# Fused attention, soft mixture and MLP on one core: logits by 256-token products, a zero block written once, w2 in 4 KB pieces, and another order of the stages

## The chip, the cores and the metric

One Trainium2 chip, one core. The metric is the device time of one execution in microseconds (us), lower is better. The kernel before took 661.55 us (median of 3 runs, 656.04 to 662.62).

## The reference

Three layers in a row, in float32. All shapes are fixed: 8 batches, 8 heads, 576 positions, head width 64, so 4608 tokens of width 512; the mixture has 8 experts with 4 slots each (32 slots).

```python
k_p = k.reshape(B, H, 72, 8, D).mean(3); v_p = v.reshape(B, H, 72, 8, D).mean(3)
attn = softmax(q @ k_p.T / 8)                 # 576 x 72 for each batch and head
x = (attn @ v_p) as (4608, 512)
logits = x @ phi                              # 4608 x 32
d = softmax(logits, axis=0)                   # over the tokens
slot_input = d.T @ x                          # 32 x 512, 4 slots for each of 8 experts
slot_out[e] = relu(slot_input[e] @ w1[e]) @ w2[e]
x = softmax(logits, axis=1) @ slot_out
out = (s * relu(x @ w_in) ** 2 + b) @ w_out   # width 2048 inside
```

## The kernel before, in words

The order on every engine is written out by hand; each engine runs its own list from front to back. Strings at the top of the file (`LOOP`, `FIRST`, `TAIL`, `BEHIND`, `PLAN1`, `PLAN2`, `KEEP`) hold that order.

**Attention loop (L703).** The 4608 tokens are 36 tiles of 128, nine for each pair of batches; tile 0 of nine (jj = 0) takes the last 64 tokens of both batches. Letters stand for steps of a tile, and a string for each pass names which step of which tile comes when: A transposes q (L363), B makes the scores (L387) and takes the row maximum off (L391, L393), C does exp and the normalisation (L401 on ACT, L402 on DVE, L422 on POOL), D transposes the probabilities P (L441, and L449 for the last 64 of the 576 rows), E makes the logits (L467), F transposes them back (L480) and writes them into L (L488). x is never formed: the logits are P times `vpf`, which is the pooled v times phi (576 rows x 32 slots, as four blocks of 128 rows and one of 64). E and F work once for two tiles, on 256 tokens, so 16 times, and once for each jj = 0 tile, so 4 times.

- Step E before: four quarters of 64 tokens, five blocks of rows. Each of the 20 products has a 128 x 32 weight (`vpf`) and 64 moving columns, and quarter g writes partitions 32g to 32g + 31. A float32 product is two matmul instructions, and each has its own weight load, so the trace counts 40 and 40. ACT copies 128 x 64 out (L471), one transpose brings it back (L480), two DVE copies put it into L (L488).
- The fifth block of `vpf` has 64 empty rows, which a POOL memset (L332, in `v_prep3`) clears for each pair of batches.
- `p` in a string advances `prep`, which pools k and v of the next pair (`PLAN1`, `PLAN2`: `k` or `v`, `d` for DVE or `g` for POOL, and the chunk; a capital is a transpose, L275), then L316, L336 and L305. `r` advances `dispatch`, the softmax over the tokens of one batch and its slot inputs (L539 to L614: a maximum by L539, L546 and L548, the difference by L551 and L553, exp at L555, products at L579, transposes at L594, L601 and L606). `w5` is five warm-up products on a constant (L252).

**Tail (L768).** The last steps and the last two dispatches (`6` and `7`), with the merging of the eight batches (`m`, M2, M3, M4), in the order of `TAIL`. It ends with L616, which writes the slot inputs `siz`.

**Expert stage (L975).** 32 pieces of 1 MB, half an expert each, in the order `EORD`: w1 products at L984 (32 slot columns as weight, 256 moving columns of w1, four column groups), w2 products at L993. `hidden` copies the sums (L948), transposes them (L954) and applies relu (L961). `BEHIND` says what is put behind which piece: `t` transposes combine weights (L932, and copies on ACT at L936), `c` their halves, `i` and `o` start a conversion of a block of w_in or w_out to the narrower format (`narrow`, L818: five DVE steps L825 to L835, L837 on ACT, L838 and L839 on POOL). A conversion is advanced by one stage behind each following piece, and its ACT step stands in ACT's list where that happens.

All loads are issued by SP in one order (`pump`), each when a buffer is free. `KEEP` says behind which pieces a ring buffer is kept as scratch, not given back.

**End of the expert stage (L1030).** The slot sums are copied (L1033), transposed in one go (L1034), and copied out of the one PSUM bank by ACT and DVE, two quarters each (L1036).

**MLP (L1212).** 96 steps, each with 18 products of 512 columns at L1139 and, for a later step, two at L1079. In the last group the sums are added into `part` by DVE (L1152), six tiles for a block, and SP writes them out (L1155).

Of the kernel before, what the change touches and what calls it, by code (L numbers as in the profile page):

```python
# [10 lines left out]
F32 = mybir.dt.float32  # L11
# [3 lines left out]
ALU = mybir.AluOpType  # L15
AX = mybir.AxisListType
# [3 lines left out]
WIPOS, WOPOS = 26, 26  # L20


BEHIND = {12: 't0 c3 t1', 20: 'o1', 9: 'c0 c1', 17: 'i1', 16: 't2', 18: 'o0 t3', 15: 'i0', 23: 't4', 10: 'c2', 28: 't5'}
TAIL = "6 C4 D2 F0 E2 X1 6 W3 6 6 6 F2 D3 m D4 W1 6 E4 6 m 7 m 7 F4 7 W2 7 7 M2 6 7 7 X2 M3 6 M4 W3 7 X3 7"
BUSY = 2
CUT = 1

LOOP = (
# [9 lines left out]
)  # L38
FIRST = {
# [8 lines left out]
}  # L48
PREP = (4, 10, 19)
PLAN1 = "kd1 kg0|kg0|kg2|K0 kd1 kg2 vg0|vg0 K1 vg2|vg2 K2 V0 vd1 vd1|V1 V2"  # L50
PLAN2 = "kg2|kg2 kg0|kg0 kg1 K2||kg1|vg2 vg2 K0|vg0|vg0 K1|V2 vg1 V0 vg1|V1"
NRING, NRAW = 10, 3
LTB = 1
KEEP = (1, 4, 6, 7)
XR = (3, 2, 1, 2)

W_MAX = 122879.9921875
# [3 lines left out]
def kernel(  # L61
# [23 lines left out]
    NG = 6  # L85
# [6 lines left out]
    ident = cpool.tile([128, 128], F32, name="ident")  # L92
# [19 lines left out]
    def plan(key, shape_str, src, n, **kw):  # L112
        loads.append((key, shape_str, src, n, kw))
# [74 lines left out]
    for w, e, hf in EORD[:BRIEF] + EORD[BRIEF + NBRIEF:NSLOT] + EORD[BRIEF:BRIEF + NBRIEF] + EORD[NSLOT:]:  # L188

        if (w, e, hf) == EORD[WIPOS]:  # L190
            plan_wi(0)
        if (w, e, hf) == EORD[WOPOS]:
            plan_wo(0)
        if w == "w1":
            plan((w, e, hf), "p (c f) -> p c f", w1[e, 256 * hf:256 * hf + 256, :].rearrange("(c p) f -> p c f", p=128), 2048, c=2)
        else:
            plan((w, e, hf), "p (c d) -> p c d", w2[e, 512 * hf:512 * hf + 512, :].rearrange("(c p) d -> p c d", p=128), 2048, c=4)
    for n in (1, 2):
        plan_wi(n)
    for n in (1, 2):  # L200
# [7 lines left out]
    ap1 = actx.enter_context(tc.tile_pool(name="ap1", bufs=1, side="right"))  # L208
# [43 lines left out]
            nc.tensor.matmul(out=ps[:, 0:128], lhsT=ident, rhs=ident, start=True, stop=True)  # L252

    vt_t, vps_t, vpf_t = {}, {}, {}
    kvp = {}

    def pool_chunk(nm, pr, c, eng):
# [69 lines left out]

    def v_prep3(pr):
        vpt = vpt_t.pop(pr)
        vpf = (ap1 if pr % 2 else apb).tile([128, 5, 2, 32], F32, tag="vpf", name="vpf")  # L330
        vpf_t[pr] = vpf
        nc.gpsimd.memset(vpf[64:128, 4], 0.0)  # L332
        ps = bank()
        for c in range(5):
            n = min(128, PQ - 128 * c)
            nc.tensor.transpose(out=ps[0:n, 64 * c:64 * c + 64], in_=vpt[:, 128 * c:128 * c + n], identity=ident[0:64, 0:64])  # L336
        nc.scalar.copy(out=vpf[:, 0:4], in_=ps[:, 0:256].rearrange("p (c b s) -> p c b s", c=4, b=2))
        nc.scalar.copy(out=vpf[0:64, 4], in_=ps[0:64, 256:320].rearrange("p (b s) -> p b s", b=2))
# [117 lines left out]
    def st_E(t):  # L456
        pr, jj = divmod(t, 9)
        if not place(t)[1]:
            return
        assert held.pop()[1] == t  # L460
        vpf = vpf_t[pr]
        ps = bank()
        quarters = [(bb, t, bb) for bb in range(2)] if jj == 0 else [(0 if jj < 5 else 1, t - 1 + g // 2, g % 2) for g in range(4)]
        for c in range(5):
            for g, (bb, u, y) in enumerate(quarters):
                z = PT[:, c, u % 3, 64 * y:64 * y + 64] if c < 4 else PT4[:, 64 * g:64 * g + 64]
                nc.tensor.matmul(out=ps[32 * g:32 * g + 32, 0:64], lhsT=vpf[:, c, bb, :], rhs=z, start=(c == 0), stop=(c == 4))  # L467
        n = 32 * len(quarters)
        LT = apc.tile([128, 64], F32, tag="LT", name="LT", bufs=LTB)
        LT_t[t] = LT  # L470
        nc.scalar.copy(out=LT[0:n], in_=ps[0:n, 0:64])  # L471

    def st_F(t):
        pr, jj = divmod(t, 9)
        if not place(t)[1]:
            return
        L = L_t[pr]
        n = 64 if jj == 0 else 128
        ps = bank()
        nc.tensor.transpose(out=ps[0:64, 0:n], in_=LT_t.pop(t)[0:n], identity=ident[0:n, 0:n])  # L480
        for y in range(2):
            r = slice(64 * y, 64 * y + 64)
            if jj == 0:
                nc.vector.tensor_copy(
                    out=L[r, 5 * y:5 * y + 6:5, :], in_=ps[0:64, 32 * y:32 * y + 32].unsqueeze(1).to_broadcast([64, 2, 32])
                )
            else:
                nc.vector.tensor_copy(  # L488
                    out=L[r, SLOT[jj] - 1:SLOT[jj] + 1, :], in_=ps[0:64, 0:128].rearrange("p (x y s) -> p y x s", x=2, y=2)[:, y]
                )  # L490


    def merge_1():
# [481 lines left out]
    for n_, key in enumerate(EORD):  # L975
        w_, e, hf = key
        g, ge = divmod(e, EG)
        w = where[key][2]
        if w_ == "w1":
            for c in range(2):  # L980
                kc = 2 * hf + c
                wc = w[:, c].rearrange("p (i c f) -> p c i f", i=2, c=4)
                for x in range(4):
                    nc.tensor.matmul(  # L984
                        out=l1[g][32 * x:32 * x + 32, 0:256],
                        lhsT=siz[:, 128 * e + 32 * kc:128 * e + 32 * kc + 32],
                        rhs=wc[:, x],
                        start=(ge == 0 and kc == 0), stop=(ge == EG - 1 and kc == 3),
                    )
        else:  # L990
            for c in range(4):
                for x in range(4):
                    nc.tensor.matmul(  # L993
                        out=so_ps[32 * x:32 * x + 32, 0:128],
                        lhsT=h1z_of(g, 4 * hf + c)[:, 36 * ge + 16 - 4 * e:36 * ge + 48 - 4 * e],
                        rhs=w[:, c, 128 * x:128 * x + 128],
                        start=(e == 0 and hf == 0 and c == 0), stop=(e == E - 1 and hf == 1 and c == 3),
                    )
        done(key, sum(n_ >= x for x in KEEP))
        if n_ == BRIEF + NBRIEF - 1:  # L1000
            brctx.close()
# [12 lines left out]
        for x in BEHIND.get(n_, "").split():
            f = int(x[1:])
            if x[0] in "ct":
                next((combine_hl if x[0] == "c" else combine_t)(f))
            else:
                todo.appendleft(conv_wi(f) if x[0] == "i" else islice(wo_[f], 2))
        if key != EORD[-1]:  # L1020
            step_convs()
# [6 lines left out]

    busy(l1[1][:, 0:128], BUSY)
    so = si_all[:, 0].rearrange("p c s -> p (c s)")  # L1030
    sot_ps = ps_1.tile([128, 4, 32], F32, tag="hps", name="sot_ps")
    sot = cv.tile([128, 4, 4, 32], F32, name="sot")
    nc.scalar.copy(out=so, in_=so_ps[:, 0:128])  # L1033
    nc.tensor.transpose(out=sot_ps.rearrange("p c s -> p (c s)"), in_=so, identity=ident)  # L1034
    for x, copy in enumerate((nc.scalar.copy, nc.vector.tensor_copy)):
        copy(out=sot[:, 2 * x:2 * x + 2], in_=sot_ps[:, 2 * x:2 * x + 2].unsqueeze(2).to_broadcast([128, 2, 4, 32]))  # L1036
    while convs:
        advance(convs)
    ectx.close()
# [241 lines left out]
```

## Time and profile before

| | |
|---|---|
| median of 3 runs | 661.55 us (656.04 to 662.62) |
| profiled execution | 662.91 us |
| its span (first to last instruction) | 661.1 us |
| mean granted TensorE clock | 0.984 of full |
| busy share of the span: PE, PE weight loads, DVE, ACT, POOL | 94%, 78%, 69%, 61%, 45% |

The profile is of one execution. The 1.8 us between its span and its time lie outside the instructions. PE is the matmul side of TensorE and PEld its weight loads. "Idle before" is time in which an engine stood still ahead of an instruction, with the instruction that released it; "issue" means that nothing in the profile had to be waited for.

### The profile page before, as it was taken

The numbers are of one execution on the slowest core, as the hardware profiler recorded it, in microseconds if no ns is written. First come the engines' busy times: TensorE is split into PE (matmuls) and PEld (weight loads), VectorE is DVE, ScalarE is ACT, GpSimd is POOL, SyncE is SP. The second block draws the span as 40 slices with busy tenths as digits, with TensorE's granted clock in tenths as the row PEclk, the third lists the DMA queues.
The fourth block names the chain that finished last, engine by engine and source line by source line (L and its number), as shares of the span: only waits on it lengthen the run. The fifth ranks groups of instructions, "written<-read, shape, count | busy, mean of one in ns | idle before, by whom it ended". The sixth has DMA issues, their size and how long they took to land.

```text
span 661.1 us, 14418 instructions
## 1 busy us (share of the span) xinstructions
PE 620.4 (94%) x5907; PEld 512.6 (78%) x5907; DVE 456.0 (69%) x740; ACT 401.5 (61%) x659; POOL 300.5 (45%) x240
## 2 busy tenths in 40 slices
PE   5777899999798899999999999999999999999996
PEld 5566777878567688888888888888888888888885
DVE  3778776869757677885777879886657555666443
ACT  2567576756164688866566666565566665555561
POOL 1788897723105334632333353343315241999000
PEclk9989998989898999999999999999999999999999
DMA  8999976756999310211202103011000000232222
GB/s 285 403 335 326 362 234 236 254 196 246 331 382 387 122 64 2 64 63 56 72 1 65 63 1 100 28 65 65 0 1 0 1 1 1 96 95 96 96 96 95
DMA packets 41329, 89.06 MB, mean 135 GB/s; under 512 B 6960, under 2 KB 15152, under 8 KB 41264
## 3 DMA queue, kind: packets, MB, share of 16 engines
q1 hardware_dynamic: 41264, 88.16, 38.3%
q8 instruction: 46, 0.75, 0.5%
q14 instruction: 19, 0.16, 0.1%
HBM read 78.71 MB, written 9.44 MB: 133 GB/s over the span
## 4 chain that ended last, share of the span: by engine, by line
PE 83%; DVE 7%; DMA 4%; issue 2%; SPq 1%; ACT 1%; POOL 1%; DVEq 0%; POOLq 0%; ACTq 0%
PE o L1139 59%; PE h L1079 5%; PE sc L387 3%; PE w L363 2%; PE w L441 2%; PE w L467 2%; PE so_ps L993 1%; DMA ring<-in_q_dram 1%; DMA qm<-in_q_dram 1%; PE l L984 1%; DMA raw<-in_moe_w_in_dram 1%; PE w L579 1%; PE w L275 1%; SPq L230 1%; DVE S L393 1%
## 5 line engine op out<-in xcount | busy, mean ns | idle before, releaser
L1139 PE MATMUL o<-whi,gh 128*128 128x512 f32 x576 | 225.2, 391 | 0.6 <-DVE gh L1065 0.6
L1139 PE MATMUL o<-wlo,gh 128*128 128x512 f32 x576 | 224.8, 390 | 0.0
L1139 PE MATMUL o<-whi,gl 128*128 128x512 f32 x576 | 209.2, 391 | 0.0
L1107 DVE TENSOR_TENSOR gl<-r,gh 128x768 fp32r<-128x768 f32 (+1 forms) x97 | 104.8, 1081 | 115.2 <-ACT gh L1099 113.9
L1091 ACT ACTIVATE r<-h 128x768 f32<-128x768 f32 x94 | 76.7, 816 | 141.1 <-PE h L1079 139.0
L838 POOL TENSOR_TENSOR fr<-fr,xp 128x512 f32<-128x512 f32 x28 | 45.3, 1618 | 178.9 <-ACT fr L837 156.5
L1139 PEld LDWEIGHTS o<-whi,gl 128*128 128x128 f32 x576 | 108.0, 188 | 22.9 <-DVE gl L1107 0.2
L1139 PEld LDWEIGHTS o<-whi,gh 128*128 128x128 f32 x576 | 108.1, 188 | 21.3 <-issue 1.4
L1139 PEld LDWEIGHTS o<-wlo,gh 128*128 128x128 f32 x576 | 108.2, 188 | 19.0
L1152 DVE SCALAR_TENSOR_TENSOR part<-o,sb_t,part 128x512 f32<-128x512 f32 x144 | 96.9, 741 | 3.2 <-PE o L1139 3.1
L1092 ACT ACTIVATE r<-r 128x768 f32<-128x768 f32 x94 | 79.7, 848 | 3.0
L1099 ACT CAST gh<-r 128x768 fp32r<-128x768 f32 x94 | 78.5, 835 | 2.6
L1250 POOL TENSOR_TENSOR part<-part,wsum 128x512 f32<-128x512 f32 x36 | 53.3, 1524 | 15.1 <-ACT wsum L1244 15.1
L422 POOL TENSOR_TENSOR P<-S,sm 128x576 f32<-128x576 f32 x32 | 36.7, 1151 | 33.8 <-DVE sm L404 24.6
L1079 PE MATMUL h<-cT,S 128*128 128x384 f32 x192 | 49.5, 338 | 0.7 <-DVE S L1172 0.7
L1079 PEld LDWEIGHTS h<-cT,S 128*128 128x128 f32 x192 | 35.9, 188 | 9.2 <-issue 1.1
L402 DVE TENSOR_REDUCE sm<-S 128x8 f32<-128x584 f32 x36 | 27.2, 756 | 14.5 <-ACT S L401 14.3
L391 DVE TENSOR_REDUCE mx<-sc 128x8 f32<-128x576 f32 x36 | 26.5, 735 | 13.7 <-PE sc L387 13.2
L365 ACT COPY qT<-w 128x512 f32<-128x512 f32 x36 | 21.0, 584 | 17.5 <-PE w L363 13.1
L387 PE MATMUL sc<-kb,qT 64*64 64x72 f32 x1152 | 28.3, 237 | 3.2 <-issue 3.2
L393 DVE TENSOR_TENSOR S<-sc,mx 128x576 f32<-128x576 f32 x36 | 27.3, 758 | 4.0 <-POOL P L422 0.6
L387 PEld LDWEIGHTS sc<-kb,qT 64*64 64x64 f32 x1152 | 22.5, 139 | 8.9 <-issue 6.6
(235 smaller groups left out, 856.7 us busy)
## 6 DMA issues: line engine op xcount, KB each, us to landing
ring<-in_moe_w_dram SPq DMA_DIRECT2D x15, 1024.0 KB, 7.2
x<-in_moe_w_dram SPq DMA_DIRECT2D x11, 1024.0 KB, 8.0
raw<-in_moe_w_in_dram SPq DMA_DIRECT2D x8, 1024.0 KB, 5.4
raw<-in_moe_w_out_dram SPq DMA_DIRECT2D x8, 1024.0 KB, 4.9
out_dram<-part SPq DMA_DIRECT2D x32, 256.0 KB, 2.6
ring<-in_q_dram SPq DMA_DIRECT2D x7, 1024.0 KB, 14.8
ring<-in_k_dram SPq DMA_DIRECT2D x9, 768.0 KB, 10.1
ring<-in_v_dram SPq DMA_DIRECT2D x7, 768.0 KB, 12.8
```

The source lines that it names most:

```text
L387: nc.tensor.matmul(out=sc[r, x, KP * i:KP * i + KP], lhsT=qT[p, i, r], rhs=kb[p, n, :], start=True, stop=True)
L393: nc.vector.tensor_tensor(out=S[:, :, :, 0:KP], in0=scv, in1=mx.unsqueeze(3).to_broadcast([128, 2, 4, KP]), op=ALU.subtract)
L422: nc.gpsimd.tensor_tensor(out=o, in0=S, in1=rb, op=ALU.mult)
L838: nc.gpsimd.tensor_tensor(out=fr, in0=fr, in1=xp, op=ALU.mult)
L1079: nc.tensor.matmul(out=h[x][:, 0:384] if i == 0 else h[:, x, 0:384], lhsT=Sw[:, f, :], rhs=cT(c, 384), start=True, stop=True)
L1091: nc.scalar.activation(out=r, in_=h[:, :, 0:384], func=ACTF.Relu)
L1092: nc.scalar.activation(out=r, in_=r, func=ACTF.Square)
L1099: nc.scalar.copy(out=gh_t[i], in_=r)
L1107: nc.vector.tensor_tensor(out=gl[:, x], in0=r[:, x], in1=gh[:, x].bitcast(F32), op=ALU.subtract)
L1139: nc.tensor.matmul(out=o_t[tt], lhsT=l[:, x, 128 * c:128 * c + 128], rhs=r, start=(fi == 0 and n == 0), stop=(fi == GROUPS[g] - 1 and n == 1),
L1152: nc.vector.scalar_tensor_tensor(out=p, in0=o_t[tt], scalar=sb_t[:, 0:1], in1=p, op0=ALU.mult, op1=ALU.add)
L1250: nc.gpsimd.tensor_tensor(out=p, in0=p, in1=wsum, op=ALU.add)
```

## The change

Step E takes each block of rows as one product with all 256 tokens. The four full blocks go into the four column groups; the fifth block is cut into four pieces of 64 tokens (16 at jj = 0), one added to each group. So a pair of tiles has 8 products (16 matmuls, 16 weight loads). The four groups then hold partial sums: ACT copies 128 x 256, two transposes of 128 x 128 bring them back, and one DVE reduction adds the four. At jj = 0 there are 16 products (32 and 32), one transpose, one reduction and two small copies. Two `vpf` tiles are made at the start and cleared there by DVE. Pieces of w2 have two runs of 4 KB in each partition where there were four of 2 KB; w1's columns are read with a step of two elements, so that the hidden rows come in the same order. The slot sums are transposed in two halves into two banks. In the last MLP step the six tiles are finished one after the other. The strings are new.

```diff
-BEHIND = {12: 't0 c3 t1', 20: 'o1', 9: 'c0 c1', 17: 'i1', 16: 't2', 18: 'o0 t3', 15: 'i0', 23: 't4', 10: 'c2', 28: 't5'}
-TAIL = "6 C4 D2 F0 E2 X1 6 W3 6 6 6 F2 D3 m D4 W1 6 E4 6 m 7 m 7 F4 7 W2 7 7 M2 6 7 7 X2 M3 6 M4 W3 7 X3 7"
+BEHIND = {12: 't0 c3 t1', 9: 'c0 c1', 18: 'o0 t2 t3', 23: 't4', 10: 'c2', 28: 't5', 14: 'i0', 22: 'o1', 15: 'i1'}
+TAIL = "6 C4 D2 F0 6 E2 6 X1 F2 6 D3 6 m D4 6 6 E4 7 m 7 F4 6 7 7 7 m M2 7 7 X2 M3 W2 7 6 M4 7 X3 W3"
 LOOP = (
-    "C B r E A D F",
+    "F C B E A D r",
     "B p F r C E D A r",
-    "r r F E r C A B D p",
+    "r r F r C B E D A p",
...
 FIRST = {
-    2: "p r D r r r r E C A r F B r r p r w5",
+    2: "r D p r r r r r E C r F A r B r p",
...
-PLAN1 = "kd1 kg0|kg0|kg2|K0 kd1 kg2 vg0|vg0 K1 vg2|vg2 K2 V0 vd1 vd1|V1 V2"
-PLAN2 = "kg2|kg2 kg0|kg0 kg1 K2||kg1|vg2 vg2 K0|vg0|vg0 K1|V2 vg1 V0 vg1|V1"
+PLAN1 = "kg0 kd1 kg0||kg2|K0 kd1 kg2 vg0|vg0 vg2 K1 vg2|K2 V0 vd1 vd1|V1 V2"
+PLAN2 = "kg2|kg2 kg0|kg0 kg1 K2||kg1|vg2 vg2 K0||vg0 vg0|V0 V2 vg1 K1 vg1|V1"
-KEEP = (1, 4, 6, 7)
+KEEP = (1, 3, 5, 7)
...
-            plan((w, e, hf), "p (c d) -> p c d", w2[e, 512 * hf:512 * hf + 512, :].rearrange("(c p) d -> p c d", p=128), 2048, c=4)
+            src = w2[e, 512 * hf:512 * hf + 512, :].rearrange("(a p c) d -> p a (c d)", a=2, c=2)
+            plan((w, e, hf), "p (a x) -> p a x", src, 2048, a=2)
...
+    vpf_b = [p.tile([128, 5, 2, 32], F32, name=f"vpf{i}", bufs=1) for i, p in enumerate((apb, ap1))]
+    for vpf in vpf_b:
+        nc.vector.memset(vpf[64:128, 4], 0.0)
...
-        nc.gpsimd.memset(vpf[64:128, 4], 0.0)
...
-        quarters = [(bb, t, bb) for bb in range(2)] if jj == 0 else [(0 if jj < 5 else 1, t - 1 + g // 2, g % 2) for g in range(4)]
-        for c in range(5):
-            for g, (bb, u, y) in enumerate(quarters):
-                z = PT[:, c, u % 3, 64 * y:64 * y + 64] if c < 4 else PT4[:, 64 * g:64 * g + 64]
-                nc.tensor.matmul(out=ps[32 * g:32 * g + 32, 0:64], lhsT=vpf[:, c, bb, :], rhs=z, start=(c == 0), stop=(c == 4))
+        for bb, r in parts(0) if jj == 0 else [(0 if jj < 5 else 1, slice(0, 256))]:
+            for c in range(4):
+                z = PT[:, c, t % 3, r] if jj == 0 else PT[:, c, ::-2] if t % 3 == 0 else PT[:, c, t % 3 - 1:t % 3 + 1]
+                nc.tensor.matmul(out=ps[32 * c:32 * c + 32, r], lhsT=vpf[:, c, bb, :], rhs=z, start=True, stop=False)
+            m = (r.stop - r.start) // 4
+            for g in range(4):
+                rg = slice(r.start + m * g, r.start + m * g + m)
+                nc.tensor.matmul(
+                    out=ps[32 * g:32 * g + 32, rg], lhsT=vpf[:, 4, bb, :], rhs=PT4[:, rg], start=False, stop=True
+                )
...
-        nc.tensor.transpose(out=ps[0:64, 0:n], in_=LT_t.pop(t)[0:n], identity=ident[0:n, 0:n])
...
+        for x in range(k_):
+            nc.tensor.transpose(out=ps[:, 128 * x:128 * x + 128], in_=LT[:, 128 * x:128 * x + 128], identity=ident)
+        s0 = SLOT[jj] - k_ + 1
+        nc.vector.tensor_reduce(
+            out=L[:, s0:s0 + k_, :], in_=ps[:, 0:128 * k_].rearrange("p (x g s) -> p x s g", x=k_, g=4),
+            axis=AX.X, op=ALU.add,
+        )
...
-                wc = w[:, c].rearrange("p (i c f) -> p c i f", i=2, c=4)
+                wc = w[:, c].rearrange("p (i a f c) -> p a c i f", i=2, a=2, c=2)
...
-    nc.tensor.transpose(out=sot_ps.rearrange("p c s -> p (c s)"), in_=so, identity=ident)
+    for x in range(2):
+        r = slice(64 * x, 64 * x + 64)
+        nc.tensor.transpose(out=sot_ps[x][:, 0:64], in_=so[r], identity=ident[r, r])
...
+        if i == len(steps) - 1:
+            for tt in range(NG):
+                st_o(i, (tt,), (0, 2, 1))
+            break
```

## Rows read from the trace of the kernel before

**Rows 1.** By stage: us, PE, PEld, DVE, ACT, POOL busy, PE clock, DMA share, GB/s:

```profile
0.00:58.00 58.00, 40.72 (x657) 33.65 (x661) 39.94 (x65) 29.51 (x65) 35.60 (x36) 0.94 0.99 347
58.00:160.00 102.00, 93.76 (x2175) 77.41 (x2171) 77.32 (x173) 71.42 (x177) 68.81 (x65) 0.97 0.74 250
160.00:177.30 17.30, 13.18 (x234) 10.72 (x232) 12.27 (x40) 4.38 (x14) 2.98 (x3) 0.90 0.95 354
177.30:217.00 39.70, 35.25 (x795) 26.68 (x796) 26.29 (x51) 19.64 (x45) 12.62 (x11) 0.96 1.02 374
217.00:661.10 444.10, 437.50 (x2060) 364.19 (x2060) 300.23 (x416) 276.58 (x360) 180.50 (x126) 1.00 0.15 51
```

**Rows 2.** PE's waits between 58 and 160 us: for whom, total, times, longest:

```profile
PE sc L387 <- issue: 2.6, 2, 1.3
...
PE w L316 <- issue: 2.4, 2, 1.4
...
PE w L579 <- issue: 1.5, 1, 1.5
```

**Rows 3.** Two stretches from the end of one issue wait to the next:

```profile
66.83:73.94 7.11, 5.63 (x127) 4.88 (x127) 4.32 (x9) 4.10 (x10) 5.43 (x7) 1.00 1.01 412
...
97.00:103.11 6.11, 4.80 (x128) 3.82 (x128) 3.80 (x9) 3.90 (x10) 6.03 (x6) 1.00 0.70 197
```

**Rows 4.** The stretch behind the wait that ended at 103.11 us:

```profile
103.11:107.50 4.39, 4.39 (x41) 3.95 (x41) 1.52 (x2) 2.26 (x6) 2.45 (x4) 0.63 1.02 415
```

**Rows 5.** The chain that ended last: start, us, what:

```profile
80.48 0.69 PE w L467 x40
...
100.10 0.44 PE w L363 x4
...
177.33 7.98 PE l L984 x144
```

**Rows 6.** Groups by line and shape: count, busy, mean ns, idle before:

```profile
L471 ACT COPY LT<-w 128x64 f32<-128x64 f32 x16 | 3.3, 208 | 2.4 <-PE w L467 2.1
...
L454 ACT COPY PT<-w 64x256 f32<-64x256 f32 x16 | 5.9, 367 | 0.0
...
L488 DVE COPY L<-w 64x64 f32<-64x64 f32 x32 | 7.0, 218 | 0.2
...
L391 DVE TENSOR_REDUCE mx<-sc 128x8 f32<-128x576 f32 x36 | 26.5, 735 | 13.7 <-PE sc L387 13.2
```

**Rows 7.** Groups by line and shape, two ACT lines of 512 elements:

```profile
L837 ACT ACTIVATE fr<-raw 128x512 f32<-128x512 uint32 x28 | 18.7, 668 | 0.0
...
L895 ACT CAST whi<-th 128x512 fp32r<-128x512 f32 x5 | 3.1, 617 | 0.8 <-POOL th L839 0.8
```

**Rows 8.** PE in order of time, 30 to 47 us, two waits:

```profile
34.88 0.31 PE L467 MATMUL w<-PT,vpf 128*32 128x64 f32 x4 [1.44 <-POOL vpf L332]
...
45.75 0.68 PE L363 MATMUL w<-ident,qm 128*128 128x128 f32 x4 [1.48 <-DMA qm<-in_q_dram]
```

**Rows 9.** All engines in order of time in the tail:

```profile
168.65 0.40 PE L551 MATMUL w<-ident,md 32*128 32x32 f32 x2 [1.24 <-DVE md L548]
...
170.51 2.13 PE L579 MATMUL w<-P,dd 128*32 128x144 f32 x32
...
173.26 0.19 DVE L567 COPY z_all<-w 128x32 f32<-128x32 f32 x1 [2.82 <-PE w L566]
```

**Rows 10.** ACT and PE in order of time in the expert stage:

```profile
204.85 0.67 ACT L837 ACTIVATE ring<-raw 128x512 f32<-128x512 uint32 x1 [3.25 <-POOL ring L839]
...
205.42 0.23 ACT L961 ACTIVATE ring<-hps 128x96 f32<-128x96 f32 x1
...
205.75 0.52 PE L993 MATMUL so_ps<-ring,ring 128*32 128x128 f32 x10 [2.18 <-POOL ring L839]
```

**Rows 11.** DVE at the end of the expert stage:

```profile
216.44 0.42 DVE L1036 COPY sot<-sot_ps 128x256 f32<-128x256 f32 x1 [5.81 <-ACT sot L1036]
```

**Rows 12.** DVE at the end of the kernel:

```profile
652.95 4.04 DVE L1152 SCALAR_TENSOR_TENSOR part<-o,sb_t,part 128x512 f32<-128x512 f32 x6 [3.10 <-PE o L1139]
```

More of the change, by code (lines that the diff above doesn't have):

```diff
@@ L329, in v_prep3 @@
         vpt = vpt_t.pop(pr)
-        vpf = (ap1 if pr % 2 else apb).tile([128, 5, 2, 32], F32, tag="vpf", name="vpf")
-        vpf_t[pr] = vpf
-        nc.gpsimd.memset(vpf[64:128, 4], 0.0)
+        vpf = vpf_t[pr] = vpf_b[pr % 2]
         ps = bank()
@@ L460, in st_E @@
         assert held.pop()[1] == t
+        n_ = 128 if jj == 0 else 256
         vpf = vpf_t[pr]
         ps = bank()
-        quarters = [(bb, t, bb) for bb in range(2)] if jj == 0 else [(0 if jj < 5 else 1, t - 1 + g // 2, g % 2) for g in range(4)]
-        for c in range(5):
-            for g, (bb, u, y) in enumerate(quarters):
-                z = PT[:, c, u % 3, 64 * y:64 * y + 64] if c < 4 else PT4[:, 64 * g:64 * g + 64]
-                nc.tensor.matmul(out=ps[32 * g:32 * g + 32, 0:64], lhsT=vpf[:, c, bb, :], rhs=z, start=(c == 0), stop=(c == 4))
-        n = 32 * len(quarters)
-        LT = apc.tile([128, 64], F32, tag="LT", name="LT", bufs=LTB)
+        for bb, r in parts(0) if jj == 0 else [(0 if jj < 5 else 1, slice(0, 256))]:
[8 more added lines that the diff above has]
+                )
+        LT = apc.tile([128, 256], F32, tag="LT", name="LT", bufs=LTB)
         LT_t[t] = LT
-        nc.scalar.copy(out=LT[0:n], in_=ps[0:n, 0:64])
+        nc.scalar.copy(out=LT[:, 0:n_], in_=ps[:, 0:n_])
     def st_F(t):
@@ L477, in st_F @@
         L = L_t[pr]
-        n = 64 if jj == 0 else 128
+        LT = LT_t.pop(t)
+        k_ = 1 if jj == 0 else 2
         ps = bank()
-        nc.tensor.transpose(out=ps[0:64, 0:n], in_=LT_t.pop(t)[0:n], identity=ident[0:n, 0:n])
[L481 to L490, printed above, removed]
+        for x in range(k_):
[5 more added lines that the diff above has]
+        )
+        if jj == 0:
+            nc.vector.tensor_copy(out=L[0:64, 0, :], in_=L[0:64, 5, :])
+            nc.vector.tensor_copy(out=L[64:128, 10, :], in_=L[64:128, 5, :])
     def merge_1():
@@ L986 @@
                         lhsT=siz[:, 128 * e + 32 * kc:128 * e + 32 * kc + 32],
-                        rhs=wc[:, x],
+                        rhs=wc[:, x // 2, x % 2],
                         start=(ge == 0 and kc == 0), stop=(ge == EG - 1 and kc == 3),
@@ L995 @@
                         lhsT=h1z_of(g, 4 * hf + c)[:, 36 * ge + 16 - 4 * e:36 * ge + 48 - 4 * e],
-                        rhs=w[:, c, 128 * x:128 * x + 128],
+                        rhs=w[:, c // 2, 512 * (c % 2) + 128 * x:512 * (c % 2) + 128 * x + 128],
                         start=(e == 0 and hf == 0 and c == 0), stop=(e == E - 1 and hf == 1 and c == 3),
@@ L1030 @@
     so = si_all[:, 0].rearrange("p c s -> p (c s)")
-    sot_ps = ps_1.tile([128, 4, 32], F32, tag="hps", name="sot_ps")
+    sot_ps = [p.tile([128, 512], F32, tag=z, name="sot_ps") for p, z in ((ps_1, "hps"), (ps_l, "l1"))]
     sot = cv.tile([128, 4, 4, 32], F32, name="sot")
     nc.scalar.copy(out=so, in_=so_ps[:, 0:128])
-    nc.tensor.transpose(out=sot_ps.rearrange("p c s -> p (c s)"), in_=so, identity=ident)
+    for x in range(2):
+        r = slice(64 * x, 64 * x + 64)
+        nc.tensor.transpose(out=sot_ps[x][:, 0:64], in_=so[r], identity=ident[r, r])
     for x, copy in enumerate((nc.scalar.copy, nc.vector.tensor_copy)):
-        copy(out=sot[:, 2 * x:2 * x + 2], in_=sot_ps[:, 2 * x:2 * x + 2].unsqueeze(2).to_broadcast([128, 2, 4, 32]))
+        z = sot_ps[x][:, 0:64].rearrange("p (c s) -> p c s", s=32)
+        copy(out=sot[:, 2 * x:2 * x + 2], in_=z.unsqueeze(2).to_broadcast([128, 2, 4, 32]))
     while convs:
```

26 rows, old and new, of tables (FIRST, LOOP) are left out of this document.

## The prediction

> **What bounds the kernel now.** I read four views in this order: the busy times by stage, PE's waits inside each stage, the timeline across each wait, and the groups by shape for prices.
>
> By stage [rows 1] the MLP takes 444.1 us with PE busy for 437.5 of them at full clock. The change touches only its last step, so those 444 us stay. Everything else must come out of the first 217 us. There the stretch from 58 to 160 us is PE's: 93.8 of 102.0 us busy, DVE at 77.3 and ACT at 71.4. The expert stage (177.3 to 217) looks bound by DMA (share 1.02), but PE is busy for 35.3 of 39.7 us, and no wait of PE there names a DMA. The start, up to 58 us, has PE at 40.7 of 58 beside a full DMA (0.99); it goes at the pace of arriving q, k and v and of their pooling.
>
> The waits inside 58 to 160 are the surprise. The three largest entries say "issue" [rows 2]: 2.6 + 2.4 + 1.5 = 6.5 us in five waits of 0.9 to 1.5 us. PE waits for nothing that the profile shows, in the middle of runs of equal products. The instruction counts show a pattern: from the end of one such wait to the end of the next lie 127 + 127 and 128 + 128 matmuls and weight loads [rows 3]. So PE stops at places about 256 instructions apart: its instructions arrive in blocks, and a block is late when the one before is used up quickly. The stretches are 7.11 and 6.11 us long and hold 1.48 and 1.31 us of waiting, so PE used up those blocks in 5.6 and 4.8 us. [...]
>
> **The change part by part.** The sum is made against the profiled execution (662.91 us, of which 1.8 lie outside the span), 1.4 us above the median of 661.55; the difference that comes out is then taken off the median.
>
> *Steps E and F on PE.* Before, E is 40 matmuls in 0.69 us [rows 5], 17 ns each. After, it has 8 of 256 columns in four column groups and 8 of 64. The nearest row is w1's products, 256 columns in four column groups: 7.98 / 144 = 55 ns [rows 5]. So 8 x 55 + 8 x 17 = 580 ns, 0.11 us less. F gets a second transpose, and four take 0.44 us [rows 5], so 0.11 us more. The sum is zero for each of the 16 pairs. If only one half came about, it would be 1.8 us either way. At jj = 0 there are 12 matmuls more, at 17 ns 0.2 us, 0.8 us for the four at most. I take 0.
>
> *Steps E and F elsewhere.* ACT's copy grows from 208 ns towards 367 ns, that of a 256-column copy [rows 6]: 16 x 0.16 = 2.6 us. It lies beside PE, and ACT has 30 us free of the 102. LT has one buffer, so this copy stands between E and F; what queues behind it on ACT is the next P and q copies. If that cover were gone, it would cost the 2.6 us. DVE loses two copies of 218 ns and gains one reduction of 256 elements; 735 ns for 576 [rows 6] gives 0.33 us by proportion, and with a fixed part up to 0.45. Nothing taken.
>
> *Fewer instructions.* For each pair 24 matmuls and 24 weight loads go and one transpose (2 instructions) comes: 46 fewer; jj = 0 adds 24. In 58 to 160 us there are 13 pairs and 3 such tiles: 13 x 46 - 3 x 24 = 526 of 2175 + 2171, or 12%. Blocks of 254 are 17.1 before and 15.0 after. Without the 6.5 us of waits the stretch takes 95.5 us, so a block lasts 5.6 us before and 6.4 after. Each late block gains some 0.8 us to arrive in: five waits shrink by about 4. Because a burst of other steps can fall on a block's end just as before, I take -3.5, with 0 and -6.5 as ends. With shorter stops some of the 3.1 us at the low clock should go too; I take -1.3, with ends -3.1 (all) and +1.6 (one more such stretch).
>
> [...]
>
> *The zero rows.* E waits 1.44 us for POOL's memset of `vpf` in the first pair [rows 8]; that goes. But 10 us later PE waits 1.48 us for a DMA, which would then last longer. I take 0, ends -1.4 and 0. The new memsets run at the start, where DVE waits for k.
>
> *New strings in the loop and the start.* `w5` and the moved steps of `PLAN1` lie where PE waits for loads; I take 0, with 2 us either way. `KEEP` hands two ring buffers back one w1 piece later (16 x 55 ns = 0.9 us), and SP's list then waits for a buffer of another pool; 0.
>
> *Tail.* PE waits 1.24 us for the maximum L548 of the last batch [rows 9], behind the third part of `m` on DVE; in the new string that part comes after the difference. Then 32 products take 2.13 us at the low clock, and DVE waits 2.82 us for what follows them while `6` and W3 stand ahead of the last transposes [rows 9]. The new string puts these transposes ahead of `6`'s last step. All three could give 4 us; half the warm-ups go too, and another low clock costs 1.6. I take -2.0.
>
> *Expert stage.* Relu (L961) stands in ACT's list behind L837 of conversion `o1`, which waits 3.25 us for POOL; PE waits 2.18 us for the relu (the wait is booked on the same POOL step) [rows 10]. In the new string `o1` starts behind piece 22, so its L837 comes after the relu. PE has its transposes done before this, so the wait goes: -2.2, ends 0 and -3.9 (a low clock behind it). Next late are the last pieces of w2, and there the 4 KB runs help. The best rate of these rows is 415 GB/s, when w1 with its 4 KB runs was arriving [rows 4], against 374 in the stage [rows 1], so w2's 16.8 MB could save 4.4 us of transfers; PE waits for none, so 0.
>
> *w1 with a step of two.* No PE row has such a moving operand. On ACT the input with a step of two takes 668 ns, the packed one 617 [rows 7], 8% more. On its 256 matmuls of 55 ns that is 0 to 1.1 us; if each column cost double, 14.2. I take 0, the nearest engine's row being small; 14.2 stays as the far end.
>
> *Slot sums.* DVE's copy starts 0.4 us after ACT's, having waited for it in the same bank [rows 11]; with two banks they run together, less a second transpose (0.11): -0.3.
>
> *Last step.* The six DVE sums take 4.04 us in a row and start after the fifth product [rows 12]. One by one they start two products earlier and keep up with PE: -0.4.
>
> Sum: -3.5 - 1.3 - 2.0 - 2.2 - 0.3 - 0.4 = -9.7; 662.91 becomes 653.2, and on the median 661.55 - 9.7 = **652**.
>
> **The rivals.** *The blocks are not the cause, or the stops only move.* Then fewer instructions give nothing: -4.9 remain, 656.6. For it: the stops hit different steps, as chance would have it. Against it: the equal counts.
>
> *All stops of the loop go.* -6.5 and -3.1 in place of -3.5 and -1.3, and the tail's whole 4 in place of 2: 4.8 + 2.0 more, -16.5, 645. For it: a block gains 0.8 us where waits are 0.9 to 1.5. Against it: two are longer than 1.4.
>
> *The step of two slows w1's products.* PE is the bound of the expert stage, so each ns on 256 matmuls is 0.256 us; from 38 ns more (93 instead of 55) the whole gain is gone. At double, 661.55 - 9.7 + 14.2 = 666. [...] Against it: ACT's 8%. [...]
>
> *The new order gains nothing.* Tail, expert stage and clock are given back by new waits; 658 to 663.
>
> **How the numbers follow.** A measurement of this kernel can tell about 1% (6.6 us), so faster means under 654.9. Forecast (647 to 657): 0.54, of which a fifth is not under 654.9. Blocks not the cause: 0.16, a quarter of it under. All stops gone: 0.12. Step of two: 0.09, half of it over 668.2. No gain: 0.09, a fifth of it slower. Faster: 0.43 + 0.04 + 0.12 = 0.59; slower 0.06; the rest 0.35. The range of 644 to 661 leaves out some 0.06 below and 0.13 above.
>
> **What would show it.** Right: L467 counts 384 instead of 720; its x16 stands at 0.55 to 0.6 us in the chain; "issue" of PE between 58 and 160 under 3.5 us, stops still about 256 apart; no POOL wait at L993; the expert stage under 38 us. Wrong: w1's x144 over 8.5 us, "issue" still above 6, or the tail above 17 us.

## The result and the profile after

The changed kernel takes 653.28 us (median of nine runs, 651.31 to 654.33) beside 661.55 us of the kernel before (nine runs, 653.63 to 662.86). The medians are 8.3 us apart; the ratio of the two kernels' times is 0.990, 95% interval 0.9861 to 0.9939, which is 6.6 us. The profiled execution of the changed kernel took 651.54 us with a span of 649.8, 11.3 us shorter than before's 661.1, where 9.7 were forecast. That is more than the timings give: before's trace is of an execution of 662.91 us, above all nine of its runs, and the changed kernel's 651.54 us is next to the least of nine. Differences read between the two traces are too large by some 3 to 5 us in sum.

The stages of the changed kernel, cut at the start of the last score product, of the first w1 product and of the first product with the slot sums ([rows 1] makes its second cut 3.9 us after the first of these); us, PE, PEld, DVE, ACT, POOL busy, granted PE clock, DMA share, GB/s:

```profile
0.00:58.00 58.00, 42.74 (x605) 34.34 (x609) 41.90 (x66) 30.08 (x64) 34.88 (x35) 0.85 0.99 349
58.00:148.20 90.20, 86.54 (x1875) 69.80 (x1879) 74.44 (x157) 69.95 (x170) 67.90 (x62) 1.00 0.81 276
148.20:166.40 18.20, 14.88 (x249) 11.27 (x238) 15.76 (x44) 7.81 (x21) 4.01 (x4) 1.00 0.85 324
166.40:206.90 40.50, 36.19 (x796) 26.70 (x796) 25.47 (x51) 19.48 (x45) 12.66 (x11) 0.96 1.01 389
206.90:649.80 442.90, 437.38 (x2060) 364.31 (x2060) 300.11 (x416) 276.78 (x361) 181.13 (x126) 1.00 0.15 50
```

Before, the last score product started at 156.1 us, the first of w1 at 177.3 and the first with the slot sums at 217.0. So the loop gives 7.9 us (156.1 to 148.2), the tail 3.0 (21.2 to 18.2), the expert stage takes 0.8 back (39.7 to 40.5), and what follows it gives 1.2 (444.1 to 442.9). The loop's gain comes in steps: with tile 12 of 36 the changed kernel is 2.2 us ahead, with tile 22 it is 6.3, and these are the places where before had its stops. Tiles 8 to 11, just ahead, are level to 0.6 us (tiles are counted from 0).

PE's waits of the changed kernel between 58 and 150 us, to be read beside [rows 2]:

```profile
PE w L279 <- issue: 0.7, 1, 0.7
PE w L451 <- DVE si_all L623: 0.6, 1, 0.6
...
PE w L615 <- issue: 0.2, 1, 0.2
PE sc L389 <- issue: 0.2, 1, 0.2
```

The 6.5 us of "issue" (6.9 with a small stop behind 150 us) have become 1.1, and the clock of this stretch, 0.97 before, is 1.00. The groups of steps E and F and of w1 (L469 and L475 are E's products, L480 ACT's copy, L493 the reduction, L993 w1), from the stretches 58 to 150 and 160 to 210:

```profile
L469 PE MATMUL w<-PT,vpf 128*32 128x256 f32 x96 | 7.7, 391 | 0.5 <-ACT vt L298 0.5
...
L480 ACT COPY LT<-w 128x256 f32<-128x256 f32 x12 | 4.4, 370 | 2.4 <-PE w L475 2.3
...
L493 DVE TENSOR_REDUCE L<-w 128x64 f32<-128x256 f32 x11 | 4.2, 381 | 0.0
...
L498 DVE COPY L<-L 64x32 f32<-64x32 f32 x3 | 2.5, 820 | 0.1
...
L993 PE MATMUL l<-ring,siz 128*32 128x256 f32 x144 | 8.8, 390 | 0.1
```

And the chain that ended last, one E of the loop (start, us, what):

```profile
98.60 0.57 PE w L469 x8
99.17 0.11 PE w L475 x8
```

E takes 0.57 + 0.11 = 0.68 us on PE, before 0.69 [rows 5]: the products themselves gain nothing. F's second transpose makes it dearer: from the start of F to PE's next product it is 0.31 us in place of 0.20 (medians at the full clock). So a pair of tiles costs PE some 0.1 us more than before. ACT's copy (370 ns) and DVE's reduction (381) came out as taken from [rows 6]. L498, one of two small copies at jj = 0, was not expected to take 0.8 us for 32 elements; it lies beside PE (the last section has what the trace shows of it).

The expert stage, PE's waits between 166 and 207 us:

```profile
PE so_ps L1002 <- issue: 2.7, 2, 2.2
PE hps L963 <- ACT si_all L957: 1.0, 1, 1.0
PE o L889 <- DVE sot L1048: 0.6, 1, 0.6
```

The wait for POOL [rows 10] is gone as meant. In its place w2's products stop for "issue", 2.7 us in two stops. The timeline has the larger:

```profile
199.82 0.42 PE L1002 MATMUL so_ps<-raw,ring 128*32 128x128 f32 x8 [2.22 <-issue]
```

Its block of instructions began at 193.74 us and held 3.86 us of work for PE.

Why the loop gained and the expert stage did not is what the runs had to settle. The theory, the author's reading of the counts in [rows 3]: PE's instructions arrive in blocks of 256, a late block stops PE, and what matters is how many instructions each step puts through. The rivals: E and F's own work got cheaper in another way, or the new order carries the gain.

### The profile page after: what moved, and what is told of

Same layout as the page of the kernel before. It is cut to its first block, busy times and chain, and to the rows that moved or that the text cites. A ratio compares the mean times of both kernels' runs of the same rounds, so it can differ in the third digit from the quotient of the medians.

```text
span 649.8 us, 13708 instructions
## 1 busy us (share of the span) xinstructions
PE 617.7 (95%) x5566; PEld 506.4 (78%) x5566; DVE 457.7 (70%) x730; ACT 404.1 (62%) x659; POOL 300.6 (46%) x236
## 4 chain that ended last, share of the span: by engine, by line
PE 80%; DVE 9%; POOL 4%; ACT 3%; issue 2%; DMA 1%; SPq 1%; DVEq 0%; POOLq 0%; ACTq 0%
PE o L1151 60%; PE h L1091 5%; PE so_ps L1002 2%; PE sc L389 2%; PE l L993 2%; PE w L443 2%; PE w L365 2%; POOL P L424 1%; DVE sm L404 1%; DVE S L395 1%; DMA ring<-in_q_dram 1%; DVE mx L393 1%; POOL ring L264 1%; DVE part L1164 1%; PE w L279 1%
```

## The experiments

Each run's ratio is to the kernel before, timed beside it; the changed kernel itself has 0.990. Times in the table are from each run's trace: "issue" is the sum of such waits of PE from 58 us to the last score product, then the start of that product, the length of the tail and of the expert stage. In e2 and e6 one more stop of the loop (1.5 and 1.3 us) stands at a block's end but is put down to POOL by the trace, so it is not in the sum.

| run | ratio (95%) | issue | last scores | tail | expert stage |
|---|---|---|---|---|---|
| before | 1 | 6.9 | 156.1 | 21.2 | 39.7 |
| changed | 0.9900 (0.9861 to 0.9939) | 1.1 | 148.2 | 18.2 | 40.5 |
| e1_cols64 | 0.9962 (0.9934 to 0.9989) | 3.4 | 152.9 | 19.9 | 40.3 |
| e1_cols128 | 0.9846 (0.9818 to 0.9875) | 0.9 | 147.7 | 18.5 | 43.4 |
| e2_before_EF | 1.0042 (1.0007 to 1.0077) | 1.5 | 153.8 | 22.2 | 44.7 |
| e3_after_oldloop | 0.9913 (0.9880 to 0.9946) | 2.6 | 152.4 | 18.0 | 39.5 |
| e4_oldtail | 0.9949 (0.9926 to 0.9971) | 0.7 | 148.3 | 21.9 | 43.0 |
| e5_oldbehind | 0.9926 (0.9904 to 0.9947) | 2.4 | 151.0 | 18.7 | 42.6 |
| e6_oldw | 0.9899 (0.9866 to 0.9932) | 0.7 | 150.3 | 18.1 | 40.8 |
| e7_w2groups | 0.9904 (0.9869 to 0.9939) | 2.7 | 151.4 | 18.1 | 40.6 |
| e8_after_oldEF | 0.9970 (0.9937 to 1.0003) | 5.1 | 149.7 | 19.5 | 40.3 |
| e9_before_scores128 | 0.9986 (0.9957 to 1.0016) | 0 | 152.0 | 19.7 | 41.0 |
| e10_after_scores128 | 1.0023 (0.9989 to 1.0056) | 0.3 | 154.0 | 17.9 | 42.6 |
| e11_after_scores128_w2groups | 1.0013 (0.9981 to 1.0045) | 0.5 | 157.8 | 17.7 | 40.4 |

One trace is one execution: e4 to e7 have the loop of the changed kernel word for word, and their last scores come 0.1 to 3.2 us after its own, mostly because a single stop (0.7 to 1.8 us at 63 to 65 us) comes in some executions and not in others. The loops of e10 and e11 are the same as well, and their last scores lie 3.8 us apart. The loop of one trace is good to some 3 to 4 us, the ratios by their intervals to 0.2 to 0.4%, or 1.5 to 2.6 us.

**More instructions for the same products: e1_cols64, e1_cols128.** E's 256-column products cut into four of 64 columns, or two of 128.

```diff
-            for c in range(4):
...
-                nc.tensor.matmul(out=ps[32 * c:32 * c + 32, r], lhsT=vpf[:, c, bb, :], rhs=z, start=True, stop=False)
+            pieces = 1 if jj == 0 else 4
+            for i_ in range(pieces):
+                for c in range(4):
...
+                        y = (c * 4 // 4 + 1 + i_) % 4
+                        o_ = slice(64 * y, 64 * y + 64)
...
+                    nc.tensor.matmul(out=ps[32 * c:32 * c + 32, o_], lhsT=vpf[:, c, bb, :], rhs=z, start=True, stop=(i_ < pieces - 1))
```

> The kernel after, with each 256-column product of step E cut into four of 64 columns (jj > 0): the same columns and the same result, 40 matmuls and 40 weight loads for a pair instead of 16 and 16, as before the change; step F, the order and all else as after. Theory (instruction blocks come too late): PE's waits for nothing, about 256 instructions apart, return between 58 and 150 us, 4 to 7 us in sum, some with the low clock behind them; with 1.8 us for the shorter products (0.11 us for each of 16 pairs) the kernel is 5 to 9 us above after. Rival (the new order of the strings took the waits away): only the 1.8 us, waits under 2 us.

> As the run with 64 columns, but cut in two: products of 128 columns, 24 matmuls and 24 weight loads for a pair, no more column time. Theory (blocks): a block lasts some 0.3 us less than in after, so 0.5 to 2 us of waits return; the kernel 0.5 to 3 us above after. Rival (order): no difference, within 0.5 us.

The 64-column version, with E's old count of 40 matmuls a pair and otherwise the changed kernel, loses 0.0062 x 661 = 4.1 us of the 6.6, a little under the 5 to 9 expected, and stops are back. PE's waits in 58 to 150 us:

```profile
PE w L443 <- issue: 1.5, 3, 0.9
...
PE w L595 <- issue: 1.1, 1, 1.1
...
PE w L622 <- issue: 0.8, 2, 0.4
```

They hit P's transposes (L443), the dispatch's products (L595) and its last products (L622), none of them a step that was edited: only the place at which a block ends has moved. The 128-column version (24 matmuls) costs nothing in the loop, 0.9 us of stops, where 0.5 to 2 us and a longer time were expected. So the loss does not grow evenly with the count.

**E and F alone, and all but E and F: e2_before_EF, e8_after_oldEF.** The kernel before with the new E and F (and the zero rows as before), and the changed kernel with the old E and F.

```diff
-        quarters = [...]
-        for c in range(5):
-            for g, (bb, u, y) in enumerate(quarters):
+        for bb, r in parts(0) if jj == 0 else [(0 if jj < 5 else 1, slice(0, 256))]:
+            for c in range(4):
...
```

> The kernel before with the new steps E and F alone (old strings, old loads, zero rows by POOL). Theory (blocks): most of the loop's gain is there, 4 to 8 us below before, PE's issue waits between 58 and 155 us down from 6.5 to under 3. Rival (order): within 1.5 us of before, as E and F cost PE the same time.

> The changed kernel with steps E and F as before (64-token products, two DVE copies), everything else as changed, the new order too. Theory (PE's instructions come in blocks of 256, a late block stops PE; E and F's fewer instructions make blocks last longer): the stops in 58 to 150 us come back, some 5 to 8 us in all with the low clock behind them, as in the run with 64 columns a product (+6); time 6 to 8 us above the changed kernel, about 658 to 660. Rival (the new order alone carries the gain, E and F only matter inside the old order): within 2 us of the changed kernel.

In the new order the old E and F cost 0.0070 x 661 = 4.6 us (6 to 8 were expected), and the stops stand on E itself (PE's waits, then PE in order of time, 58 to 150 us):

```profile
PE w L469 <- issue: 4.5, 5, 1.6
...
PE w L320 <- issue: 0.3, 1, 0.3
...
PE w L443 <- issue: 0.3, 1, 0.3
```

```profile
64.78 0.52 PE L469 MATMUL w<-PT,vpf 128*32 128x64 f32 x18 [0.60 <-issue]
...
72.49 0.75 PE L469 MATMUL w<-PT,vpf 128*32 128x64 f32 x19 [1.03 <-issue]
...
78.62 0.65 PE L469 MATMUL w<-PT,vpf 128*32 128x64 f32 x30 [0.56 <-issue]
```

From each of these ends to the next lie (columns as in the stages above):

```profile
64.77:72.49 7.72, 6.68 (x125) 5.50 (x126) 6.13 (x12) 5.99 (x16) 6.50 (x6) 1.00 1.02 414
72.49:78.62 6.13, 5.57 (x127) 4.48 (x127) 4.33 (x12) 3.06 (x7) 5.37 (x6) 1.00 1.04 352
```

These rows do not count PE's semaphore instructions. With them, 255 and 257 records lie from stop to stop: 256 again. Counted over all of PE's records from the first one on, every "issue" stop over 0.4 us between 16 and 215 us stands at a remainder of 193 or 194 modulo 256, in before (eight stops, from 43.55 to 192.52 us), changed (three, from 94.85 to 199.82 us) and all variants; a few of 0.3 us do not.

Two things in this trace differ from before's. The granted clock of its loop (58 to 149.7 us) is 1.00: 5.1 us of stops, one of 1.60 us, brought no low clock. And its last scores come only 1.5 us after the changed kernel's, with 4.0 us more of stops. The trace is of an execution of 654.07 us, where the median of ten is 657.89, so the 4.6 us rest on the timings; one trace does not show where all of them lie.

In the old order the new E and F shorten the loop by 2.3 us and cut its "issue" from 6.9 to 1.5, yet the kernel is no faster (0.0042 x 661 = 2.8 us slower, where 4 to 8 us faster were expected). What the loop gave was lost further on. PE's waits of e2_before_EF in its expert stage:

```profile
PE so_ps L1000 <- issue: 3.6, 4, 2.9
...
PE l L991 <- issue: 0.8, 1, 0.8
```

Before had 0.5 us of "issue" there. With fewer instructions ahead, every later block ends at another step, and here one ended among w2's products. In the loop, too, one stop of 1.5 us was left, which the trace puts down to POOL (L260) though it stands at a block's end, and the clock around it was low:

```profile
108.00:118.74 10.74, 9.22 (x128) 7.33 (x128) 8.07 (x16) 3.60 (x9) 7.98 (x8) 0.68 0.57 199
```

So E and F alone, and the rest alone (-2.0 us in e8), do not add up to the -6.6 of both.

**The count of instructions in another step: e9_before_scores128.** The kernel before, with one score product of 128 tokens for two of 64.

```diff
-                for y in range(2):
-                    r = slice(64 * y, 64 * y + 64)
+                for y in range(1 if u else 2):
+                    r = slice(0, 128) if u else slice(64 * y, 64 * y + 64)
```

> The kernel before with one thing else: for the 32 steps whose keys are the same for both halves of the tokens, one score product of 128 tokens in place of two of 64. That is 16 products and 16 weight loads fewer in each such step, more than E and F's cut (46 per pair of steps before the change, here up to 64), and in a step that the change does not touch. Theory: it is the count of PE instructions that matters, not what E and F do: no stop over 1 us in 58 to 156 us, last scores at 147 to 150 us instead of 156.1, and the time 5 to 8 us under that of the kernel before. Rival 1 (the gain belongs to E and F's own products, transposes and copies): within 2 us of before. Rival 2 (as when E and F alone were changed): the loop gains 2 to 6 us, but late blocks in the expert stage take most of it back; 0 to 3 us under before.

The stops are gone without E or F being touched: PE's waits between 58 and 150 us have no entry at all, for "issue" or anything else, and PE is busy for 93.90 of the 94 us to the last scores. But the time did not follow: the ratio can't be told from 1. The expectation had left the products' own price out. The score products (58 to 148 us), of before and then of this run:

```profile
L387 PE MATMUL sc<-kb,qT 64*64 64x72 f32 x736 | 17.5, 232 | 2.6 <-issue 2.6
```

```profile
L387 PE MATMUL sc<-kb,qT 64*128 64x72 f32 x354 | 24.9, 279 | 0.0
```

Two products of 64 tokens take 2 x 17.5 / 736 = 48 ns, one of 128 takes 24.9 / 354 = 70: 22 ns more, 354 times, 8 us, against 6.9 us of stops and the low clock behind them. In this trace the last scores come 4.1 us earlier, but a loop is good to 3 to 4 us only. Why the wide product is dearer was not tried. A busy PE in place of "issue" is no gain. Nor does the run tell fewer instructions from slower ones: both make a block last longer.

**The same in the changed kernel: e10_after_scores128, e11_after_scores128_w2groups.**

> The changed kernel with the same 128-token score products. In its loop hardly any stop is left, so theory by stops alone says little can be gained there: 0 to -1.5 us. PE's own time: if 16 products and loads fewer a step spare PE some 10 ns each, 32 steps x 32 x 5 to 10 ns = 5 to 10 us of busy time, of which the part between 58 and 150 us is on the path: -3 to -6 us, if DVE and ACT (77 and 71 of 102 us before) do not become the bound. A stop in the expert stage (2.5 us) may stay or move.

> The run before this one with w2's products in four column groups side by side (fewer instructions in the expert stage). Theory: w2's rows arrive at the DMA's pace, so the block stops of the expert stage go and waits for w2's transfers take their place; within 1.5 us of the run with the 128-token scores alone. Rival: with the loop ended earlier, w1 and w2 are issued earlier as well and the stage shortens by the 2 to 3 us of the stops.

There are hardly any stops to remove here, and the price of the products stays: the ratio rises from 0.990 to 1.002, some 8 us. The expectation of e10 had the sign wrong, as it took the saved instructions for saved time. e11 adds e7's edit (below) and changes nothing more.

**The order: e3_after_oldloop, e4_oldtail, e5_oldbehind.** The changed kernel with the old strings of the loop and its start (`LOOP`, `FIRST`, `PLAN1`, `PLAN2`), of the tail, or of what stands behind the pieces; for example

```diff
-TAIL = "6 C4 D2 F0 6 E2 6 X1 F2 6 D3 6 m D4 6 6 E4 7 m 7 F4 6 7 7 7 m M2 7 7 X2 M3 W2 7 6 M4 7 X3 W3"
+TAIL = "6 C4 D2 F0 E2 X1 6 W3 6 6 6 F2 D3 m D4 W1 6 E4 6 m 7 m 7 F4 7 W2 7 7 M2 6 7 7 X2 M3 6 M4 W3 7 X3 7"
```

> The kernel after with the strings LOOP, FIRST, PLAN1 and PLAN2 of before. Theory (blocks): within 2 us of after. Rival (order): 4 to 8 us above after, with the issue waits back.

> The kernel after with the string TAIL of before. Theory (the prediction's tail term): the stretch from the last scores to w1's first product, 21.8 us before and 18.7 after, goes back by 2 to 3 us, and so does the whole. Rival: the expert stage takes it up, since the last pieces of w2 arrive no later: 0 to 1 us.

> The kernel after with the string BEHIND of before. Theory (the prediction's term of 2.2 us): the wait of 2 us ahead of the second half of w2 comes back, the whole 1 to 3 us slower. Rival (the stage was not shorter in after, 40.5 against 39.7 us, as it lost the same to a late instruction block and to a wait for the copy of the sums): within 1 us of after.

The old loop strings cost 0.0013 x 661 = 0.9 us by the ratio, within its uncertainty; its trace has two more stops (1.5 and 1.1 us) and loses 4.2 us in the loop. The old tail costs 3.2 us and puts the tail back to 21.9. Its waits (148 to 171 us):

```profile
PE w L615 <- DVE si_all L610: 1.3, 1, 1.3
PE w L560 <- DVE md L557: 1.3, 1, 1.3
PE w L555 <- DVE md L548: 1.0, 1, 1.0
```

In the changed kernel the same three are 0.9, 0.3 and 0.5 us, and its clock in the tail is 1.00 against 0.88 here. The old `BEHIND` costs 1.7 us; PE's waits in its expert stage:

```profile
PE so_ps L1002 <- issue: 2.9, 2, 2.7
PE so_ps L1002 <- POOL ring L848: 2.2, 1, 2.2
```

The wait for POOL is back, and the late block is there as well: they are independent of each other, and the new string really removes the first. In before the two did not meet: the two blocks that ended behind that wait (207.45 and 212.76 us) came in time.

Undone one by one, E and F, the tail and `BEHIND` cost 4.6 + 3.2 + 1.7 = 9.5 us, more than the 6.6 that the whole change gains. The parts do not simply add, and each of these prices is uncertain by some 2 to 3 us.

**The layout of w1 and w2, and w2's products: e6_oldw, e7_w2groups.**

```diff
-            src = w2[e, 512 * hf:512 * hf + 512, :].rearrange("(a p c) d -> p a (c d)", a=2, c=2)
-            plan((w, e, hf), "p (a x) -> p a x", src, 2048, a=2)
+            plan((w, e, hf), "p (c d) -> p c d", w2[e, 512 * hf:512 * hf + 512, :].rearrange("(c p) d -> p c d", p=128), 2048, c=4)
...
-                        rhs=wc[:, x // 2, x % 2],
+                        rhs=wc[:, x],
```

> The kernel after with w1 and w2 as before: w1's columns packed, w2 in runs of 2 KB. Theory (a step of two costs PE about 2 ns of 57 in each matmul of w1, the 4 KB runs save nothing that PE waits for): 0 to 0.6 us faster than after. Rival (the 4 KB runs carry the stage): 1 to 3 us slower, with PE waiting for w2.

> The kernel after with step E's cut applied to w2: each block of 128 hidden rows is one product of 512 columns in its own column group, so a piece takes 8 matmuls and 8 weight loads in place of 32 and 32 (768 instructions fewer in all); the four partial sums are added at the end by four products with a selection matrix in place of the two transposes, and the copy of the sums is four times as long. Theory (late blocks): the 2.7 us of waits for nothing in the expert stage fall under 0.6 and the low clock behind them (1.7 us) goes; 0.5 us is paid at the end: 2 to 4 us faster than after. Rival: PE then waits for w2's loads (DMA share 1.01): 0 to 1 us.

Four runs of 2 KB and packed columns take the same time as two runs of 4 KB and a step of two: 0.9899 beside 0.9900. w1's products by themselves are 3% quicker packed, and it doesn't matter:

```profile
L992 PE MATMUL l<-ring,siz 128*32 128x256 f32 x144 | 8.4, 380 | 0.1
```

e7 has one product of 512 columns for four of 128, which takes away 384 of w2's 512 matmuls and as many weight loads. No stop is left in the expert stage, and it is as long as before the edit (40.6 us); 2 to 4 us of gain were expected. PE's waits there:

```profile
PE so_ps L1001 <- DMA x<-in_moe_w_dram: 2.8, 2, 1.5
PE hps L963 <- ACT si_all L957: 1.1, 1, 1.1
```

With the late block gone, w2's transfer is late, by the same amount. e8, whose blocks happened to end elsewhere, shows it too:

```profile
PE so_ps L995 <- DMA x<-in_moe_w_dram: 2.5, 2, 1.4
PE hps L956 <- ACT si_all L950: 1.5, 1, 1.5
```

e3 and e4 have some of each (1.4 and 1.8, 1.2 and 1.8 us). So in the changed kernel the late block and the late transfer lie on top of each other, and neither alone is worth anything. No run beat the changed kernel by more than the measurement can tell: e1_cols128 has the lowest ratio, 0.9846, but its interval meets that of 0.9900, its trace has a span 2.6 us longer, and nothing in it is quicker but the loop, by 0.5 us (that trace is of an execution of 654.14 us, where the median of four is 652.48).

## Why the prediction was right, and where not

The forecast was 652.0 us with 644 to 661, faster over 1% at 0.59; measured 653.28, a ratio of 0.990. The sum of -9.7 stands against -11.3 between the two spans, -8.3 between the medians and -6.6 by the ratio, whose interval lets "faster over 1%" stand open. Right in the total, but with luck: between the traces the loop gave 3.1 us more than forecast and the expert stage 3.0 less, and these two misses cancel. In the loop alone the trace is nearer the rival in which all stops go. Of the signs named, L469 and L475 together count 384, "issue" is under 3.5 and the POOL wait is gone; E's 0.68 us isn't 0.55 to 0.6, and the expert stage isn't under 38. None of the signs of being wrong came: the tail is 14.3 us by the cut of [rows 1], and w1's products, which came nearest, have 8.43 us in the chain up to the same next step (7.98 in before [rows 5], the sign stood at 8.5).

- **Fewer instructions and the clock behind the stops: -3.5 - 1.3 = -4.8 forecast; -7.9 in the trace.** That the stops stand at the ends of blocks, and that their number hangs on how many instructions PE is given, is shown by e8 and cols64 (5.1 and 3.4 us of "issue" where the changed kernel has 1.1); e9 is in line with it, but its products are longer too. The size was off: the "issue" waits fell by 5.8 us (6.9 to 1.1), not 3.5, and the clock's 0.03 went altogether. Up to the last scores PE's idle time fell by 4.5 us (8.1 to 3.7, since other waits grew) and its busy time by 3.4 (90.0 to 86.5), of which 0.03 of 98 us, 2.9, is the clock's. The 3.1 us at the low clock, of which the -1.3 is a part, is 0.03 x 102 us from the mean clock of 0.97 in [rows 1], and the 1.6 us of one low stretch is 0.37 x 4.39 us from the clock of 0.63 in [rows 4]; that shorter stops, or E and F, bring the clock back was an estimate that no run shows: e8 has the stops and the full clock (1.00), e2 the new E and F and a clock of 0.68 around its stop of 1.5 us. The prediction shortened each stop by the 0.8 us that a block lasts longer. In the traces a stop mostly goes as a whole or stays. The ratio of e8 puts the price of E and F at 4.6 us, close to the sum that was forecast. The new strings explain little of the rest (0.9 us in e3); more of it is the choice of the two traces.
- **E and F on PE, ACT and DVE: 0.** Nearly. On PE only one half of the sum came about, the case that the prediction priced at 1.8 us: F's second transpose cost its 0.11 us, but E saved 0.01 (0.68 for 0.69) and not 0.11, some 1.6 us over 16 pairs. On ACT and DVE 370 and 381 ns, all of it beside PE, as said.
- **Zero rows, the start: 0.** Right in sum: early tiles come up to 2.4 us sooner or later, and tiles 8 to 11 are level. The warm-up `w5` is gone, and the stretch `23.30:33.50` then has a clock of 0.52 (1.00 in before) beside a DMA share of 1.02; it cost nothing that is left at tile 8.
- **Tail: -2.0 forecast, -3.0 in the trace, 3.2 when undone (e4).** PE's three waits fell from 3.7 to 1.7 us, and the 32 products from 2.13 us [rows 9], at a clock of 0.53, to 1.19 at 1.00, with half the warm-ups dropped. The term was mis-sized: of the possible 4 more came than was allowed for.
- **Expert stage: -2.2 forecast, +0.8 came.** This is the step that failed (the slot sums' -0.3 lies in the same stretch), and with it the line "the expert stage under 38 us". The edit did what the prediction said (e5 shows the POOL wait return without it). But the prediction named the last pieces of w2 as "next late" and still took the whole wait as gain, as PE waited for none of them in before. Two things stood ready behind the removed one, each about 2.5 us: an instruction block, stopping w2's products for 2.2 us, and behind it w2's transfer (e7 and e8). The trace of before could have told it: a DMA share of 1.02 in that stage [rows 1].
- **w1 with a step of two, w2 in 4 KB runs: 0 and 0.** Right (e6). 144 products took 8.8 us of busy time against 8.4; from the start of the first to the start of the 129th it is 7.32 us, 57 ns each, and 6.93 us, 54 ns, in before. The rival that feared a doubled column is out. Beside the packed columns of e6 (380 ns) the step of two costs 10 ns in 390.
- **Slot sums -0.3, last step -0.4.** Both as said. The two copies start together (206.34 and 206.37 us) and PE waits 0.6 us for them, where it was 1.0. From the start of the last matmul to the end it is 5.3 us for 5.7. Between the two another 0.9 us went that no step foresaw: before, PE waits 0.7 us for DVE (L1172) at 222.84 us, and after it doesn't; why was not tried.
- **The rival that the blocks are not the cause.** As to the place, it is out: the stops stand 256 instructions apart, and PE waited for 0.5 to 2.9 us there in these runs. That the instructions behind such a place arrive late is the author's reading of the counts; no trace shows them arrive. The rival's other half, that the stops only move, came true in the old order (e2: 3.6 us of "issue" at w2's products) and in the expert stage (2.7 us). Most ends of blocks cost little: of the changed kernel's fourteen between 58 and 145 us, one cost more than 0.5 us.

## What to carry to other kernels

Where "issue" waits stand in the middle of equal products, count PE's instructions from one to the next (256, or a multiple of it, in these runs), look for a step that puts many short instructions through in a row, and make it fewer and longer, but price the wide product first: the 256-column E cost PE the same as the narrow ones (0.68 us for 0.69), the 128-token score 22 ns more than two of 64. The stops moved with the edits ahead of them (in e1_cols64 to L443, L595 and L622), so judge the edit by repeated timings, and see first whether the stage behind is bound by transfers, for a stop removed there can be paid to the DMA (e7: 2.7 us of "issue" became 2.8 us of waits for w2). Before a wait is counted as gain, find the next one by removing it on paper for every resource whose share is about 1, even where PE has no wait for it yet.

## What was not expected of the hardware

The prediction had a block come late when the one before is used up quickly. In these traces a late block needed neither that nor full transfers. Before stopped for 1.45 us up to 133.75 us with nothing on the queues from 132 to 134 us (58 GB/s from 130 to 140), and e8's block of 6.7 us of work (64.77 to 72.49 us) was followed by a stop of 1.03. Other blocks ended after 4.8 us without any stop (151.28 to 156.04 us in before). PE's use of a block and the load on the queues thus don't decide alone whether it comes late, and what else does is open. What holds in all runs is the place.

The four copies at jj = 0 (L498, 64 x 32 elements, within L) took 0.66 to 1.17 us, while the copies of 64 x 64 elements out of PSUM that stood there before (L484) took 0.19. The trace shows what they meet:

```profile
139.04 1.15 POOL L424 TENSOR_TENSOR P<-S,sm 128x576 f32<-128x576 f32 x1 [2.18 <-DVE sm L406]
139.08 1.13 DVE L498 COPY L<-L 64x32 f32<-64x32 f32 x1
140.23 0.18 DVE L499 COPY L<-L 64x32 f32<-64x32 f32 x1
```

Each of the four ends 0.03 to 0.04 us after the POOL instruction that it started beside, and so does the one slow copy of the other half (L499, 1.10 us); the three that did not start beside one took 0.18 us. That POOL held them up is read from these times, and no run moved one of the two.
